# Attention and softplus feed-forward on one core: 64-column transposes, masks in the scores' tile mode, and another order of the first chunk's tasks

## The chip, the cores and the metric

The kernel runs on one core of a Trainium2 chip. Its engines each work through a queue of their own, in the order of the program: TensorE (PE in the profile) with its weight loads (PEld), VectorE (DVE), ScalarE (ACT), GpSimd (POOL) and SyncE (SP), which here only issues DMAs. The metric is device time in microseconds, the median of several runs; lower is better.

## What is computed

The reference is attention with two kinds of masks, followed by a feed-forward layer with a softplus between its two products:

```python
def _attn_ref(q, k, v):                      # 8 batches, 8 heads, 576 positions, 64 wide
    scores = scale * np.matmul(q, k.transpose(0, 1, 3, 2))
    mask_local = (rel >= 0) & (rel < stride)                      # heads 0-3, stride 32
    mask_strided = (rel >= 0) & (pos[None, :] % stride == pos[:, None] % stride)   # heads 4-7
    scores = np.where(masks, scores, -1000000000.0)
    ...
    attn = attn / (np.sum(attn, axis=-1, keepdims=True) + 1e-09)
    return np.matmul(attn, v)

def _moe_ref(x, w_in, w_out):                # x 4608 x 512, w_in 512 x 2048, w_out 2048 x 512
    h = x @ w_in
    g = np.maximum(h, 0.0) + np.log1p(np.exp(-np.abs(h)))
    return g @ w_out
```

The weights come in double precision.

## The kernel before

**Tiling.** Heads are taken in pairs, so there are 32 pairs n (4 to a batch). A query sees at most 64 keys after the host has sorted the positions, so the scores of a pair are nine chunks of 64 columns for 128 query rows, in two parts (six chunks and three). The feed-forward layer takes the 4608 tokens in nine chunks of 512, and the hidden width in 16 blocks f of 128. Each product is done with a high and a low part of both operands: 12 matmuls of 128x512 for a block of the hidden layer (`hidden`), and 12 for its share of the output (`output`).

**Staging.** The first chunk is special. Beside it the 32 weight blocks are brought into two parts, and the first eight pairs go through attention. All this stands as a list of task names, `FIRST`, written out by hand; tasks are emitted in its order, so it sets the order on every engine's queue and on SP's DMA queue. From the second chunk on, a planner (`Plan`) with costs and due times sets the order; nothing of that part is changed.

**Names in `FIRST`.** `q`, `k`, `v`, `wi`, `wo` and a number are loads; `D` lays q out (one half of the heads each, `D00` and `D01`). For a pair n and part j: `S` scores on PE, `X` row maxima on DVE, then either `Y`, `E`, `Z` (subtract, one wide exp, sums) or `x`, `E` (bias, one exp to each chunk, on ACT); `r`, `R`, `M` guard, reciprocal and normalising. `T` and `C` are transposes on PE and their copies out of PSUM (pairs 0 to 3), `P` transposes on DVE (pairs 4 to 7), `V` the product with v, `H` and `L` the high and low part of its result, which is the input x of the feed-forward layer. A weight block goes through `a` (ACT), `B`, `d`, `c` (DVE), `h` (high part) and `l` (low part). `F` is a block of the hidden layer, `A`, `Ae`, `Al`, `u` its softplus, `Gh`, `Gl` its two parts, `O` its share of the output, `y` the result; `Fa0` is the first nine matmuls of `F0`, for pairs 0 to 2. Names starting with `Q` belong to the second chunk. `ON_POOL`, `ON_VECTOR` and `ON_SCALAR` move single tasks from their usual engine.

**What matters around the change.** `F0` needs x of the first 512 tokens, so all of pairs 0 to 3 up to their `L`. PSUM is shared tightly: two buffers `ph` serve the hidden layer and the transposes `T`, one buffer `po` serves `V`. The masks (`mask_b`, 192 KB) are loaded by the first DMA on ACT's queue (L163). In the first two batches the mask is added on PE after a part's scores, by one matmul against the identity over all 128 rows (L336). A transpose group `T` (L447 to L460) zeroes its PSUM buffer and then does 12 matmuls of 32 weight columns each. The result tile `o` (L656) is taken from a pool of four buffers, also for the two halves into which the very last tile is split.

Of the kernel before, what the change touches and what calls it, by code (L numbers as in the profile page):

```python
# [33 lines left out]


FIRST = """
W q0 k0 D01 D00 S00 S01 X00 Y00 q1 D10 X01 D11 x01 E00 Z00 k1 S11 X11 E01 r0 R0 M0 q2 D21 S10
T00 wi0 D20 Y11 X10 x10 ai0 Bi0 T01 di0 k2 E11 S21 Z11 S20 E10 ci0 v0 r1 C00 R1 M1 X21 x21 C01 V00
wo2 q3 ao2 Bo2 do2 co2 D30 hi0 D31 wi2 T02 C02 X20 Y20 k3 H00 L00 ai2 Bi2 E20 ho2 Z20 T10 wi1 di2
v1 E21 r2 T11 S31 V01 X31 S30 lo2 x31 R2 wo3 C10 T12 ci2 H01 L01 X30 Y30 ai1 C11 V10 C12 hi2 E31  # L40
wo0 M2 H10 L10 li2 E30 Z30 T20 C20 li0 r3 R3 ao3 Bi1 M3 T21 V11 C21 H11 L11 wi11 ai11 Bi11 di1 T22
T32 C32 di11 v2 wi3 V20 C22 H20 ci1 ci11 hi11 L20 T31 ai3 Bi3 v3 hi1 li1 C31 T30 C30 li11 wo1 wi4
V21 H21 L21 V31 di3 wo6 ao1 Bo1 ao0 ci3 V30 H31 L31 H30 L30 Fa0 hi3 li3 do1 Bo0 co1 do0 Bo3 q4 D4
wi12 co0 F0 A0 Ae0 ho1 k5 Al0 u0 lo1 Fa1 k4 S40 ai4 wi6 X40 Bi4 x40 ho0 lo0 wi5 Gh0 ai5 wi7 Bi5 F1
A1 Gl0 ai7 Ae1 Al1 E40 do3 co3 di4 u1 Gh1 ho3 lo3 F2 A2 Ae2 Bi7 ci4 di5 O0 q5 wi10 wo5 ao5 Al2 Gl1
wi8 S41 D5 X41 ci5 x41 E41 u2 Gh2 hi5 di7 li5 F3 hi4 A3 Bo5 do5 ci7 Ae3 Al3 r4 R4 li4 co5 O1 M4
S50 X50 x50 hi7 u3 wo12 v4 F5 F4 ho5 Gl2 lo5 Gh3 Gl3 P4 E50 S51 ai6 ai8 Bi8 di8 X51 O2 wo4 ao4 Bi6
wo7 x51 di6 ci6 hi6 A5 Ae5 Al5 u5 li7 Bo4 q6 A4 E51 r5 k6 D6 V40 ci8 do4 O3 H40 L40 S60 co4 R5
wi13 Ae4 ai10 Bi10 Al4 V41 H41 li6 wi9 M5 u4 Gh4 Gl4 X60 Gh5 ho4 x60 L41 P5 F7 F6 hi8 wo15 lo4 Gl5
li8 di10 v5 O4 k7 E60 ao6 Bo6 A7 ai13 S61 A6 Ae6 V50 O5 Al6 ci10 hi10 do6 co6 u6 wo11 wo8 q7 li10  # L50
F10 Ae7 Al7 X61 ho6 ai9 u7 x61 ao7 Bo7 do7 Bi13 di13 Bi9 Gh7 Gl7 ci13 H50 L50 wo14 lo6 di9 ci9 Gh6
Gl6 F8 D7 E61 r6 S70 co7 A10 Ae10 ao8 Al10 Bo8 do8 R6 hi9 A8 wi15 u10 V51 li9 X70 x70 O6 Ae8 Al8
co8 wo9 u8 M6 H51 L51 wi14 P6 ho8 lo8 ai12 Gh8 ho7 lo7 Gl8 F11 hi13 li13 Bi12 Gh10 Gl10 wo10 ao9
Bo9 F9 O7 E70 S71 ai15 Bi15 do9 X71 co9 v6 ao10 Bo10 A9 Ae9 Al9 x71 do10 V60 H60 L60 u9 ho9 A11 q8
lo9 Ae11 Al11 u11 O8 di15 ci15 Gh11 Gh9 Gl9 di12 V61 H61 ao11 Bo11 wo13 F13 hi15 li15 E71 r7 R7 O9
co10 ho10 A13 ci12 hi12 ao13 Ae13 Al13 k8 v7 Gl11 L61 lo10 do11 F15 ao12 O10 M7 co11 li12 ho11
lo11 u13 Gh13 P7 A15 Ae15 Gl13 ai14 Bi14 di14 ci14 F12 hi14 Al15 u15 O11 q9 A12 Ae12 Al12 u12 Bo12
D8 Gh12 V70 Qa0 li14 F14 do12 co12 ho12 Gl12 lo12 O12 Bo13 do13 A14 co13 ho13 lo13 H70 L70 V71
ao14 Bo14 do14 Ae14 co14 Al14 u14 ho14 lo14 O13 H71 L71 Q1 Gh14 v8 Gl14 O14 ao15 Bo15 do15 co15
Gh15 Gl15 ho15 lo15 QA1 Qu1 Qh1 Ql1 Q0 QA0 O15 y1 Ob15 y2 y3 Qu0 Qh0 y0 Ql0 k9  # L60
# [59 lines left out]
def attention_softplus_ffn(  # L120
# [42 lines left out]
    nc.scalar.dma_start(mask_b, masks)  # L163

# [145 lines left out]
    def scores(n, part):  # L310

        b = order[n][0]
        masked = b < 2
# [8 lines left out]
        pss[n, part] = ps
        lo, hi = SPLIT[part]
        for x in range(lo, hi):
            for place in range(2):
# [2 lines left out]
                nc.tensor.matmul(  # L328
                    ps[64 * place : 64 * place + 64, 64 * (x - lo) : 64 * (x - lo) + 64],
                    lhsT=blocks_of(n)[:, c // 32].rearrange("p h l -> p (h l)"),  # L330
                    rhs=k_of(n)[:, c : c + 64],
                    start=x == lo or not masked,
                    stop=not masked,
                )
        if masked:
            nc.tensor.matmul(  # L336
                ps[:, : 64 * (hi - lo)], lhsT=ident_b, rhs=mask_of(n, part), start=False, stop=True
            )
# [103 lines left out]
    def early_transposes(n, g):  # L442

        ph = phs["t", n, g] = ps_h.tile([P, 512], F32, tag="ph", name=f"pt_{n}_{g}")[
            :, : 4 * TILE
        ]
        nc.tensor.matmul(ph, lhsT=warm[:, :P], rhs=warm[:, : 4 * TILE], start=True, stop=False)  # L447
        ph = ph.rearrange("p (h a c) -> p h a c", h=2, a=2)
        for x in range(2):
            for i in range(3):  # L450
                a = 2 * g + x
                chunk, place = (6 + a % 3, a // 3) if i == 1 else (a, i // 2)
                for c in range(2):
                    nc.tensor.matmul(
                        ph[32 * (i + c) : 32 * (i + c) + 32, :, x, 32 * i : 32 * i + 32],
                        lhsT=prob[n % 2][:, chunk, 32 * c : 32 * c + 32],
                        rhs=ident[:, 64 * place : 64 * place + 64],
                        start=False,
                        stop=x == 1 and (c == 0 or i == 2),
                    )  # L460
# [514 lines left out]
```

## Time and profile before

| | us |
|---|---|
| median of three runs (898.67 to 898.98) | 898.88 |
| the profiled execution's own time | 899.74 |
| its span on the chip | 897.5 |
| PE busy in the span | 885.0 (99%) |
| DVE busy | 601.4 (67%) |
| ACT busy | 446.9 (50%) |
| POOL busy | 60.0 (7%) |

The span runs from the first to the last instruction of the profiled execution. A share of busy time is a mean over stages with different limits: PE is at 99% over all, but in the first 35 us it waits several times, and there DVE, ACT and the DMAs are close to full. Where a row says `<-`, the name behind it is what ended the wait. Matmuls overlap, so a row's duration is longer than the distance to the next row; f32 matmuls show as two records each.

### The profile page before, as it was taken

To read this page: it belongs to the slowest core of one execution; us is meant where nothing else is said; L and a number is where in the kernel's file an instruction comes from. 1 tells how busy PE (TensorE), PEld (TensorE's weight loads), DVE (VectorE), ACT (ScalarE), POOL (GpSimd) and SP (SyncE) were. 2 spreads that over 40 slices of the span, in tenths; PEclk is the share of its full clock that TensorE was granted. 3 is DMA by queue.
4 is the path that set the end of the run, shared out by engine and by line. 5 is a ranking of instruction groups with operands and counts; after the bars stand their busy time and mean duration, and the time that the engine had idled before them with its cause. 6 is when DMAs were issued, how large, how long until landed. Compare 5 with 4: busy or idle time off the path is not lost.

```text
span 897.5 us, 14490 instructions
## 1 busy us (share of the span) xinstructions
PE 885.0 (99%) x5700; PEld 723.8 (81%) x5700; DVE 601.4 (67%) x1308; ACT 446.9 (50%) x796; POOL 60.0 (7%) x77
## 2 busy tenths in 40 slices
...
DMA packets 50084, 58.28 MB, mean 65 GB/s; under 512 B 3168, under 2 KB 35296, under 8 KB 50016
## 3 DMA queue, kind: packets, MB, share of 16 engines
...
q10 hardware_dynamic: 288, 0.33, 0.1%
...
## 4 chain that ended last, share of the span: by engine, by line
PE 86%; DVE 6%; ACT 3%; DMA 3%; issue 1%; SPq 1%; POOL 0%; ACTq 0%; POOLq 0%
PE py L647 40%; PE ph L607 39%; PE ps L328 2%; DMA ri<-in_moe_w_in_dram 2%; PE pv L484 2%; DVE pt L432 1%; PE po L484 1%; PE po L328 1%; ACT qT L256 1%; ACT prob L374 1%; DVE u L628 1%; DMA ro<-in_moe_w_out_dram 1%; DVE a_i L561 1%; DVE a_o L561 0%; DVE a_o L578 0%
## 5 line engine op out<-in xcount | busy, mean ns | idle before, releaser
L647 PE MATMUL py<-w_o,gh 128*128 128x512 f32 x1152 | 359.2, 393 | 0.1
L607 PE MATMUL ph<-x_h,w_i 128*128 128x512 f32 x1152 | 355.7, 390 | 1.0 <-DVE u L628 1.0
L619 ACT ACTIVATE u<-ph 128x512 f32<-128x512 f32 x144 | 86.4, 600 | 394.9 <-PE ph L607 391.9
L607 PEld LDWEIGHTS ph<-x_h,w_i 128*128 128x128 f32 x1152 | 215.8, 188 | 46.3 <-DVE u L628 1.6
L647 PEld LDWEIGHTS py<-w_o,gh 128*128 128x128 f32 x1152 | 213.8, 188 | 47.3 <-POOL w_o L593 0.9
L647 PE MATMUL py<-w_o,gl 128*128 128x512 f32 x576 | 224.2, 389 | 0.0
L607 PE MATMUL ph<-x_l,w_i 128*128 128x512 f32 x576 | 224.1, 389 | 0.0
L628 DVE SCALAR_TENSOR_TENSOR u<-ph,u 128x512 f32<-128x512 f32 x144 | 98.9, 688 | 171.9 <-ACT u L624 170.4
L432 DVE STREAM_TRANSPOSE pt<-prob 32x192 f32<-32x192 f32 x448 | 137.1, 314 | 6.4
L647 PEld LDWEIGHTS py<-w_o,gl 128*128 128x128 f32 x576 | 108.1, 188 | 22.8
L607 PEld LDWEIGHTS ph<-x_l,w_i 128*128 128x128 f32 x576 | 108.1, 188 | 22.6
L640 DVE TENSOR_TENSOR gl<-u,gh 128x512 fp32r<-128x512 f32 x138 | 96.1, 697 | 11.2 <-ACT gh L256 0.3
L622 ACT ACTIVATE u<-u 128x512 f32<-128x512 f32 x144 | 91.3, 634 | 4.5
L624 ACT ACTIVATE u<-u 128x512 f32<-128x512 f32 x144 | 90.9, 632 | 4.4
L256 ACT COPY qT<-prob 64x576 f32<-64x576 f32 x56 | 70.5, 1260 | 0.3
L256 DVE CAST gh<-u 128x512 fp32r<-128x512 f32 x130 | 55.4, 426 | 10.6 <-PE py L647 0.5
L391 DVE TENSOR_TENSOR prob<-ps,mask_b 128x384 f32<-128x384 f32 x24 | 13.4, 558 | 50.4 <-PE ps L328 50.4
L328 PEld LDWEIGHTS ps<-kT,qT 128*64 128x64 f32 x720 | 23.6, 137 | 11.6 <-issue 9.9
L328 PE MATMUL ps<-kT,qT 128*64 128x64 f32 x720 | 28.0, 226 | 0.3 <-ACT qT L256 0.3
L484 PE MATMUL pv<-pt,v_in 128*64 128x96 f32 x396 | 22.2, 248 | 0.0
L422 DVE TENSOR_TENSOR prob<-prob,st 128x576 f32<-128x576 f32 x28 | 21.2, 757 | 0.9
L391 DVE TENSOR_TENSOR prob<-po,mask_b 128x192 f32<-128x192 f32 x24 | 8.6, 357 | 19.3 <-ACT x_h L522 19.3
...
## 6 DMA issues: line engine op xcount, KB each, us to landing
...
prob<-in_qk_dram SPq DMA_DIRECT2D x28, 288.0 KB, 2.7
kT<-in_qk_dram SPq DMA_DIRECT2D x28, 288.0 KB, 3.0
...
```

Source lines behind the costliest of these rows:

```text
L256: (engine.copy if engine is nc.scalar else engine.tensor_copy)(dst, src)
L328: nc.tensor.matmul(ps[64 * place : 64 * place + 64, 64 * (x - lo) : 64 * (x - lo) + 64], lhsT=blocks_of(n)[:, c // 32].rearrange("p h l -> ...
L391: nc.vector.tensor_tensor(pv, sv, m, op=ALU.add)
L432: nc.vector.transpose(pt[32 * (i + c) : 32 * (i + c) + 32, h, a : a + hi - lo, 32 * i : 32 * i + 32,], src[:, lo:hi, 32 * c : 32 * c + 32],)
L484: nc.tensor.matmul(po[64 * h : 64 * h + 64, TILE * x : TILE * x + TILE], lhsT=vs[n][:, a, h, :], rhs=pt_of(n, a)[:, h, a % 2], start=True, ...
L607: nc.tensor.matmul(ph, lhsT=w32["i", f][:, half, cc * P : (cc + 1) * P], rhs=x_of(x, cc)[:, t0 : t0 + n], start=(i == 0), stop=(i == 3 * N ...
L619: nc.scalar.activation(us[c, f], phs[c, f], AF.Abs)
L622: nc.scalar.activation(u, u, AF.Exp, scale=-1.0)
L624: nc.scalar.activation(u, u, AF.Ln, bias=1.0)
L628: nc.vector.scalar_tensor_tensor(u, in0=phs.pop((c, f)), scalar=0.0, in1=u, op0=ALU.max, op1=ALU.add)
L640: engine.tensor_tensor(g, us.pop((c, f)), ghs[c, f].bitcast(F32), op=ALU.subtract)
L647: nc.tensor.matmul(py[t], lhsT=g[:, sl], rhs=w32["o", f][:, half], start=(f == 0 and n == 0), stop=(f == NFC - 1 and n == 2),)
```

## The change

There are five edits.

1. **Transposes.** In `early_transposes` a block whose 64 columns land on 64 rows in line is done by one matmul of 64 weight columns; only the block in the middle (i = 1) is still split in two of 32. A group has 8 matmuls after, 12 before.
2. **Masks.** For pairs 1 to 7 the mask is written first, by two matmuls that have 64 output rows each, and the scores are added to it. For pair 0 the two mask matmuls still follow the scores.
3. **The mask load** leaves its place at the head of ACT's queue and becomes a task `mask` in `FIRST`.
4. **The order** `FIRST` and the lists of engines are new throughout.
5. **The last half tile** of the result takes its buffer from the pool of the softplus (`u_pool`), not from the result's four.

```diff
 FIRST = """
-W q0 k0 D01 D00 S00 S01 X00 Y00 q1 D10 X01 D11 x01 E00 Z00 k1 S11 X11 E01 r0 R0 M0 q2 D21 S10
+W wi0 ai0 Bi0 di0 q0 D01 D00 ci0 q1 D11 D10 k0 q3 D30 D31 wo0 mask hi0 ao0 S00 X00 Y00 E00 S01 X01
...
 ON_POOL = """
-D10 D20 D30 ho2 r2 x31 hi11 hi3 x40 ho3 x41 hi5 x50 ho5 hi6 r5 x60 ho6 x61 x71 ho9 ho11 Gh13 hi14
-ho13 ho14
+D30 hi0 D20 x10 x21 x31 hi5 hi8 ho1 hi3 ho5 ho7 x70 hi13 Gh10 Gh13 hi15 ho12 ho13 Gh15 ho14 ho15
 """.split()
 ON_VECTOR = """
-D00 M0 M1 lo2 C12 M3 li1 li3 lo0 Gl0 lo3 Gl1 li5 li4 li7 li6 li10 Gl7 lo6 Gl6 Gl10 Gl9 li15 Gl11
-lo10 M7 Gh12 li14 Gl12 Gl14 Gh15 Gl15
+D01 D11 M0 lo0 M3 li1 C31 li2 li3 Gl0 Gh1 Gl3 li6 Gh4 Gl4 lo5 li9 lo8 Gl10 Gl9 li14 li15 Gl12 lo12
+lo13 Gh14 Gl14 lo14 Gl15 lo15
...
     mask_b = const.tile([P, 12 * 64], BF16, name="mask_b")
-    nc.scalar.dma_start(mask_b, masks)
...
+        rows = [slice(64 * place, 64 * place + 64) for place in range(2)]
+
+        def add(first):
+            for place in range(2):
+                nc.tensor.matmul(
+                    ps[rows[place], : 64 * (hi - lo)],
+                    lhsT=ident_b[:, rows[place]],
+                    rhs=mask_of(n, part),
+                    start=first,
+                    stop=not first,
+                )
+
+
+        if masked and n > 0:
+            add(True)
...
-        if masked:
-            nc.tensor.matmul(
-                ps[:, : 64 * (hi - lo)], lhsT=ident_b, rhs=mask_of(n, part), start=False, stop=True
-            )
+        if masked and n == 0:
+            add(False)
...
-        for x in range(2):
-            for i in range(3):
+
+        for i, width in ((1, 32), (0, 64), (2, 64)):
+            for x in range(2):
                 a = 2 * g + x
                 chunk, place = (6 + a % 3, a // 3) if i == 1 else (a, i // 2)
-                for c in range(2):
+                for c in range(0, 64, width):
+                    lo = 32 * i + c
                     nc.tensor.matmul(
-                        ph[32 * (i + c) : 32 * (i + c) + 32, :, x, 32 * i : 32 * i + 32],
-                        lhsT=prob[n % 2][:, chunk, 32 * c : 32 * c + 32],
+                        ph[lo : lo + width, :, x, 32 * i : 32 * i + 32],
+                        lhsT=prob[n % 2][:, chunk, c : c + width],
...
-        o = io_pool.tile([P, DM], F32, tag="io", name=f"o_{c}_{t}")[:, cols]
+        if cols.start == 0:
+            o = io_pool.tile([P, DM], F32, tag="io", name=f"o_{c}_{t}")[:, cols]
+        else:
+            o = u_pool.tile([P, 512], F32, tag="u", name=f"o_{c}_{t}")[:, : DM - cols.start]
...
+    first["mask"] = lambda: nc.scalar.dma_start(mask_b, masks)
```

What the new list does to the queues shows best at the head of the program. On SP's queue before, the loads began with q and k of the first pairs (`raw_q` and `early_l`), and the first weight block (`ri`) came sixth:

```order
L253 DMA raw_q_153<-in_qk_dram 128x576
L274 DMA early_l_92<-in_qk_dram 128x576
L253 DMA raw_q_181<-in_qk_dram 128x576
L274 DMA early_l_94<-in_qk_dram 128x576
L253 DMA raw_q_205<-in_qk_dram 128x576
L528 DMA ri_235<-in_moe_w_in_dram 128x4x128
```

In the changed program the same place in SP's queue reads:

```order
L541 DMA ri_152<-in_moe_w_in_dram 128x4x128
L251 DMA raw_q_158<-in_qk_dram 128x576
L251 DMA raw_q_163<-in_qk_dram 128x576
L272 DMA early_l_91<-in_qk_dram 128x576
L251 DMA raw_q_168<-in_qk_dram 128x576
L547 DMA ro_172<-in_moe_w_out_dram 128x512
L272 DMA early_l_93<-in_qk_dram 128x576
```

A weight block of 512 KB now goes ahead of q and k of pair 0, three q go ahead of the second k, and a second weight block (`ro`, for `wo0`) is sixth.

At the head of ACT's queue before, with the semaphores that each instruction waits for (`DMAHW` and a number are the eight semaphores that DMAs share in turn):

```order
L161 ACT_TABLE_LOAD
L163 DMA mask_b<-in_masks_dram 128x768
L208 CAST room_113<-ident_b 128x128 [waits Pool_49]
L256 COPY early_h_91<-raw_q_153 64x32x18 [waits DMAHW0_49]
L256 COPY early_h_93<-raw_q_181 64x32x18 [waits DMAHW3_49]
```

And the head of ACT's queue in the changed program:

```order
L160 ACT_TABLE_LOAD
L206 CAST room_112<-ident_b 128x128 [waits Pool_49]
L561 ACTIVATE a_i_154<-ri_152 128x512 [waits DMAHW0_49]
L254 COPY early_h_90<-raw_q_158 64x18x32 [waits DMAHW1_49]
L254 COPY early_h_92<-raw_q_163 64x18x32 [waits DMAHW2_49]
L254 COPY early_h_96<-raw_q_168 64x32x18 [waits DMAHW4_49]
L700 DMA mask_b<-in_masks_dram 128x768 [waits DMAHW5_49]
L561 ACTIVATE a_o_177<-ro_172 128x512
```

The mask's DMA moved behind four instructions that wait for loads of their own, and it waits for semaphore 5, which the sixth DMA of the program (`ro_172`) raises when it has landed.

On DVE's queue before, from its memsets on (`py` holds the scores of pair 0, `st` its statistics):

```order
L256 COPY early_h_91<-raw_q_153 64x18x32
L364 TENSOR_REDUCE st_178<-py_106 128x6
L351 TENSOR_TENSOR prob_104<-py_106,st_178 128x384
L364 TENSOR_REDUCE st_178<-py_107 128x3
L368 TENSOR_SCALAR st_178<-st_178 128x3
```

And the same place on DVE's queue in the changed program:

```order
L565 TENSOR_SCALAR a_i_154<-a_i_154 128x512
L574 SCALAR_TENSOR_TENSOR a_i_154<-ri_152,a_i_154 128x512
L254 COPY early_h_90<-raw_q_158 64x32x18
L591 SCALAR_TENSOR_TENSOR a_i_154<-ri_152,a_i_154 128x512
L254 COPY early_h_92<-raw_q_163 64x32x18
L375 TENSOR_REDUCE st_193<-py_105 128x6
L362 TENSOR_TENSOR prob_103<-py_105,st_193 128x384
L375 TENSOR_REDUCE st_193<-py_106 128x3
```

The three DVE steps of the weight block and a second copy of q stand ahead of the first row maxima now; from there on the first pairs' steps follow in much the same order as before.

More of the change, by code (lines that the diff above doesn't have):

```diff
@@ L36 @@
 FIRST = """
-W q0 k0 D01 D00 S00 S01 X00 Y00 q1 D10 X01 D11 x01 E00 Z00 k1 S11 X11 E01 r0 R0 M0 q2 D21 S10
[L38 to L59, printed above, removed]
@@ L60 @@
-Gh15 Gl15 ho15 lo15 QA1 Qu1 Qh1 Ql1 Q0 QA0 O15 y1 Ob15 y2 y3 Qu0 Qh0 y0 Ql0 k9
+W wi0 ai0 Bi0 di0 q0 D01 D00 ci0 q1 D11 D10 k0 q3 D30 D31 wo0 mask hi0 ao0 S00 X00 Y00 E00 S01 X01
+x01 k1 S11 Bo0 do0 E01 X11 Z00 q2 D20 D21 Y11 r0 S10 X10 x10 wi4 k2 S21 R0 E11 Z11 S20 M0 ai4 Bi4
+co0 di4 E10 T01 C01 T00 C00 k3 r1 ci4 T02 R1 M1 X20 ho0 v0 X21 Y20 wi1 ai1 Bi1 V00 H00 S30 C02 L00
+S31 x21 lo0 wo1 di1 E20 X31 V01 E21 Z20 H01 wi5 L01 T11 C11 li0 ai5 r2 ci1 v2 Bi5 T10 R2 X30 T12
+Y30 C10 hi4 x31 v1 wi8 wi7 V10 H10 L10 C12 M2 di5 E31 V11 ci5 H11 L11 wi2 li4 T21 E30 Z30 r3 R3
@@ new lines @@
+T20 C21 C20 T22 hi1 M3 li1 k4 ai8 Bi8 di8 V20 C22 hi5 H20 L20 T30 C30 v3 ci8 T32 ai2 Bi2 wo3 T31
+C31 wo7 V21 C32 V31 ao1 li5 H21 L21 V30 di2 q4 hi8 wi3 ai3 Bi3 li8 H30 H31 L31 Fa0 L30 F0 wi10 D4
+A0 Ae0 Al0 di3 ci2 Bo1 do1 ci3 wo4 co1 ho1 u0 Fa1 hi2 li2 hi3 S40 X40 x40 q5 ai7 wi9 Bi7 Gh0 F1
+li3 wo2 ao2 Bo2 F2 wo6 E40 S41 ao3 Gl0 do2 wi11 A2 Ae2 Al2 di7 v4 A1 Bo3 Ae1 Al1 do3 co3 u2 O0 lo1
+X41 x41 E41 ci7 hi7 co2 F3 r4 R4 M4 ho2 wo9 u1 Gh1 D5 Gl1 li7 ho3 A3 lo2 F4 k5 wo5 P4 Gh2 wi6 Ae3
+Gl2 Al3 u3 O1 S50 lo3 X50 ao4 q6 ao6 Bo6 x50 wo15 O2 Bo4 Gh3 Gl3 wi15 do4 co4 do6 wo10 wi12 V40
@@ new lines @@
+ai6 Bi6 di6 E50 S51 X51 A4 x51 ci6 co6 H40 L40 F5 Ae4 O3 Al4 u4 ho4 lo4 ai10 wi14 Bi10 hi6 li6 Gh4
+Gl4 F6 di10 ci10 D6 ai11 E51 A5 Ae5 ao5 r5 Bi11 di11 ci11 A6 R5 Bo5 do5 co5 V41 H41 L41 Ae6 Al6 u6
+M5 Al5 u5 hi11 k6 ho5 S60 X60 x60 P5 O4 ho6 lo6 hi10 li10 Gh6 Gl6 F7 E60 Gh5 Gl5 ai9 ao9 lo5 Bi9
+F8 S61 X61 v5 V50 A7 Ae7 Al7 u7 A8 Ae8 li11 di9 O5 Bo9 ci9 do9 x61 co9 F11 Gh7 Al8 u8 q7 Gl7 ao7
+H50 wo8 L50 ao8 Bo8 O6 Bo7 do7 co7 D7 A11 V51 do8 E61 r6 ho7 R6 hi9 Ae11 wi13 Al11 li9 co8 u11 k7
+S70 X70 F10 M6 H51 ho8 lo8 F9 Gh8 Gl8 ao10 x70 L51 lo7 wo12 ao12 Gh11 ho9 lo9 O7 Gl11 E70 S71 v6
```

16 lines of the change are left out of this document (11 added, 5 removed).

## The prediction

> **What bounds the kernel now.** I read the stages first (busy time in stretches of the span: PE, PEld, DVE, ACT, POOL, then the clock, the DMAs' busy share and GB/s), because a share over the whole span says nothing of the first 35 us.
>
> ```profile
> 0.00:10.00 10.00, 8.07 (x85) 4.47 (x85) 6.00 (x12) 5.01 (x9) 7.92 (x25) 1.00 0.84 278
> 10.00:20.00 10.00, 7.51 (x187) 5.45 (x187) 9.18 (x22) 9.06 (x28) 2.19 (x2) 1.00 1.07 394
> 20.00:30.00 10.00, 8.58 (x203) 6.14 (x203) 9.83 (x23) 8.80 (x29) 4.84 (x5) 1.00 1.00 344
> 80.00:120.00 40.00, 40.00 (x232) 32.16 (x231) 39.32 (x86) 32.48 (x75) 17.01 (x16) 1.00 0.33 113
> 120.00:130.00 10.00, 8.99 (x48) 6.80 (x47) 9.74 (x18) 5.57 (x9) 1.97 (x2) 1.00 0.13 36
> 130.00:897.50 767.50, 763.62 (x4560) 631.39 (x4558) 478.60 (x1049) 341.38 (x542) 5.29 (x5) 1.00 0.14 42
> ```
>
> In the lead-in PE has gaps, while DVE is 92 to 98% busy after the first ten us. From 80 us on PE is full, but for 1 us at 120 to 130 and the end of the last stretch. Next come PE's own timeline and its waits:
>
> ```profile
> PE ph L607 <- DVE u L628: 1.0, 1, 1.0
> PE ps L328 <- ACT qT L256: 0.3, 1, 0.3
> ```
>
> ```profile
> 34.09 0.72 PE L484 MATMUL pv<-early_l,room 128*64 128x96 f32 x12 [1.21 <-DVE x_l L520]
> 34.73 0.73 PE L607 MATMUL ph<-x_h,w_i 128*128 128x512 f32 x2
> ...
> 123.86 0.73 PE L607 MATMUL ph<-x_h,w_i 128*128 128x512 f32 x2 [0.99 <-DVE u L628]
> ```
>
> At 34.73 the feed-forward layer begins (`Fa0`), and behind it PE waits only twice, 0.3 and 1.0 us. So the time is **the start of `Fa0`, plus PE's work behind it, plus 1.3 us of waits, plus the tail**. What delays `Fa0` is the row above it: `V30` waited 1.21 us for an `x_l`, which is `L21` on DVE. DVE's timeline of the lead-in:
>
> ```profile
> 4.12 0.87 DVE L256 COPY early_h<-raw_q 64x576 f32<-64x576 f32 x1 [0.20 <-DMA raw_q<-in_qk_dram]
> 7.23 0.56 DVE L364 TENSOR_REDUCE st<-py 128x6 f32<-128x384 f32 x1 [2.24 <-PE py L336]
> ...
> 10.47 0.17 DVE L414 TENSOR_SCALAR st<-st 128x9 f32<-128x9 f32 x1 [0.41 <-ACT prob L374]
> ...
> 12.44 0.17 DVE L368 TENSOR_SCALAR st<-st 128x6 f32<-128x6 f32 x1
> 12.52 0.42 DVE L552 TENSOR_SCALAR a_i<-a_i 128x512 uint32<-128x512 uint32 x1
> 12.98 0.69 DVE L561 SCALAR_TENSOR_TENSOR a_i<-ri,a_i 128x512 uint32<-128x512 uint32 x1
> ...
> 13.85 1.49 DVE L578 SCALAR_TENSOR_TENSOR a_i<-ri,a_i 128x512 uint32<-128x512 uint32 x1
> ...
> 15.70 0.76 DVE L422 TENSOR_TENSOR prob<-prob,st 128x576 f32<-128x576 f32 x1
> ...
> 31.90 1.76 DVE L593 TENSOR_TENSOR w_i<-a_i,w_i 128x512 fp32r<-128x512 f32 x1
> 33.59 0.44 DVE L520 TENSOR_TENSOR x_l<-pv,x_h 128x288 fp32r<-128x288 f32 x1
> ```
>
> DVE waits 2.24 us for the first scores with their mask (`X00` at 7.23), then works without a break, 0.41 us apart, to the end of `L21` at 34.03. That is a chain of 26.8 us, and the first mask matmul starts it.
>
> **The lead-in, and the one large term.** In the new order DVE does the same things between `X00` and `L21`: all maxima, subtractions and sums of pairs 0 to 3, five weight blocks in full and the first step of a sixth, two low parts, one copy out of PSUM. Off DVE are `M1` (0.76 us in the row at 15.70) and `x10` and `x21` (0.17 each, the row at 12.44); `r2` comes to DVE at the 0.17 of the row at 10.47. So the chain loses 0.9 us and is 25.9 us long. `M1` on POOL costs more, but its result is wanted only by the transposes of pair 1, whose `L10` stands some 8 us further down DVE's queue; that covers it.
>
> The head of the chain moves much more. `X00` needs the first mask matmul, and that needs `mask_b`.
>
> ```profile
> 0.76 0.39 ACTq L163 DMA_DIRECT2D mask_b<-in_masks_dram  x1
> ```
>
> ```profile
> 3.05 6.32 DMA ri<-in_moe_w_in_dram
> ```
>
> ```profile
> prob<-in_qk_dram SPq DMA_DIRECT2D x28, 288.0 KB, 2.7
> ...
> mask_b<-in_masks_dram ACTq DMA_DIRECT2D x1, 192.0 KB, 3.5
> ```
>
> Before, the mask was issued at 0.76 and landed 3.5 us later, ahead of the scores. Afterwards its DMA waits until `wo0` has landed, the sixth load on SP's queue. When is that? Before, q0 landed at 4.1 (end of the wait in front of DVE's copy) and the sixth load, `wi0`, at 3.05 + 6.32 = 9.37: five loads, four of 288 KB and one of 512 KB, in 5.25 us. The new order puts a 512 KB load first, issued at about 0.75. Before, 480 KB (q0 and the mask side by side) took until 4.1 from about the same start, so I take 4.2. Behind it come four loads of 288 KB and one of 512 KB again: 4.2 + 5.25 = 9.4. At the 394 GB/s of the best stretch above those 1.70 MB need 4.3 us, so 8.5 is the low bound. The mask, 3.5 us after its issue, lands at 12.9.
>
> ```profile
> 5.38 1.55 PE L328 MATMUL py<-early_l,early_h 128*64 128x64 f32 x24 [0.60 <-ACT early_h L256]
> 6.86 0.34 PE L336 MATMUL py<-mask_b,ident_b 128*128 128x384 bf16 x1
> ```
>
> Before, `X00` began 7.23 - 6.86 = 0.37 us behind the mask matmul; so 13.3 against 7.23, **6.0 us later**. The scores themselves are no bound: k0 is fourth in the queue, lands near 6.9, and they end about 8.5. Nor is DVE's work put in front: `Bi0`, `di0`, `D01`, `ci0`, `D11` are 0.42 + 0.69 + 0.87 + 0.69 + 0.87 = 3.5 us from about 4.9, over by 8.5. DVE then stands idle for nearly 5 us with `X00` at the head of its queue, and PE stands at the mask matmul with all other scores queued behind it. So `L21`, and `Fa0` with it, come 6.0 - 0.9 = **5.1 us later**. The bounds: issue at 8.5 and the 2.7 us of the nearest quicker load give `X00` at 11.6, and +3.5.
>
> A sentence on a page: the Trainium skill ("DMA: Bandwidth & Descriptors", "Anatomy of one DMA") fits a DMA at about 2.0 us plus its bytes at 436 GB/s, an estimate of 2.45 us for the mask; the trace has 3.5 us, and by the page the lead-in term would be 4.1.
>
> **Transposes.** Twelve groups lose 4 of 12 matmuls each. I cost this at nothing: PE waits in the lead-in as it is, and DVE's chain sets its end. The cover is that chain; without it a group's 24 records (0.67 us by the timeline, as the one below) would become 16, up to 0.2 us each, 2.7 us in all at the very most.
>
> ```profile
> 24.47 0.67 PE L454 MATMUL pt<-room,prob 128*32 128x64 f32 x24
> ```
>
> **Masks.** Eight mask additions (pairs 4 to 7) stand between dense matmuls on PE and count in full.
>
> ```profile
> 46.68 0.39 PE L647 MATMUL py<-w_o,gl 128*128 128x512 f32 x1
> 47.00 0.57 PE L328 MATMUL ps<-kT,qT 128*64 128x64 f32 x12
> 47.50 0.26 PE L336 MATMUL ps<-mask_b,ident_b 128*128 128x192 bf16 x1
> 47.54 0.70 PE L607 MATMUL ph<-x_h,w_i 128*128 128x512 f32 x2
> 48.08 0.39 PE L607 MATMUL ph<-x_l,w_i 128*128 128x512 f32 x1
> ```
>
> Between the records at 46.68 and 48.08 lie 1.40 us; three dense records of 0.227 (0.68) leave 0.72 for scores and mask, of which the scores have 0.50 from start to mask. The mask and all changes of shape come to 0.22. Two half matmuls instead of one could run side by side and save the change in the middle (down to -0.1 us each), or one after the other (up to +0.13, half of the 0.26). I take +0.02 each, 0.2 in all; the ends are -0.8 and +1.0. The Trainium skill ("TensorEngine Tiling (Array Packing)", "Key Properties") says that changing the tiling mode drains TensorE; by that this edit saves one drain a block. The row's 0.22 leaves room for no more than the -0.8 above.
>
> **Waits behind `Fa0`.** DVE has done one weight block more by `L21` (0.42 + 0.69 + 0.69 = 1.8 us, now ahead of `X00`), and in the lists two `Gl` and `M7` leave DVE for about as much in biases and one `Gh`. It is some 2 us less behind PE than before, so the 1.0 us wait at 123.86 should go: -1.0. The other wait, 0.3, I leave.
>
> **Tail.**
>
> ```profile
> 893.66 0.42 DVE L256 COPY o<-py 128x256 f32<-128x256 f32 x1 [0.67 <-PE py L647]
> 894.38 0.37 ACT L256 COPY o<-py 128x256 f32<-128x256 f32 x1 [0.81 <-DMA out_dram<-o]
> ```
>
> The last half tile on ACT waits for a result buffer whose DMA is still under way, until 894.38; its DVE twin began at 893.66. With a buffer of its own it begins 0.7 us sooner. What is late next is the twin's own DMA, issued 0.2 us or so sooner than ACT's was: I take -0.5.
>
> **Sum**, against the profiled execution's own 899.74: +5.1 - 1.0 + 0.2 - 0.5 = +3.8, 903.5. That execution was 0.86 above the median of the three runs (898.88), so I forecast a median of **902.7 us**. A difference of about 0.2%, 1.8 us, is what a measurement of this kernel can tell from none.
>
> **The rivals.** (1) *The mask is not late* and the weight block in front pays: slower turns into no change. For it speaks that DVE has real work for the 3.5 us ahead of `X00`; against it the semaphore on which the DMA waits. If the mask lands by 8.5, `X00` follows the scores at 9.1, 1.9 later than before; less 0.9 the lead-in is +1.0, the sum -0.3, the median 898.6. Each us that the mask lands behind 8.5 adds one; from 10.6 on it is slower by over 1.8. (2) *The DVE holds go.* Two DVE operations took 1.49 and 1.76 us where their like took 0.69, while POOL was at work: 1.9 us that the new order may or may not meet again. Without them the forecast is 900.8. Against it: POOL has more large operations in the lead-in now (`M1`, `li0`, `M2`, `li4`). Together (1) and (2) give 896.7, faster. (3) *A new wait in the dense part:* in the new queue `u1` stands behind `u2` and a row of weight steps, and the fifth hidden block needs the buffer that `u1` frees; at some three weight steps late (0.69 each) this adds 2 us: 904.7. (4) *The transposes do nothing*, since the added change from 32 to 64 columns takes back what the four matmuls give; that is already the forecast's zero.
>
> **How the numbers follow.** Forecast 0.50 (nearly all of it slower, 0.04 within 0.2%: its own bounds, +3.5 for the lead-in and -0.8 for the masks, end at 900.1); (3) 0.10, slower; (2) 0.12, half slower, half same; (1) 0.16, of which 0.12 same and 0.04 faster; (1) with (2) 0.12, faster. That makes faster 0.16, same 0.22, slower 0.62. The range reaches from between the case (1) and its faster form, 897.5, to 905.0, which takes in (3).
>
> **What would show it.** Right: the first row maxima on DVE near 13.3 us with a wait of nearly 5 us before it, ended by the mask matmul or its DMA; ACT's issue of the mask near 9.4; the first 128x512 matmul of the hidden layer near 39.8; no wait for `u` near 125; ACT's last copy without a wait for a DMA. Wrong: `X00` before 11, or `Fa0` before 37. If `Fa0` is late as said and the time is not, PE's work behind it must have become shorter, and the masks would be the place to look.

## The result and the profile after

| | before | after |
|---|---|---|
| median, same chip and hour (us) | 898.93 (898.67 to 900.03) | 907.79 (907.29 to 908.44) |
| span of the profiled execution (us) | 897.5 | 906.4 |
| first row maxima, `X00` (us) | 7.23 | 15.41 |
| start of the feed-forward layer, `Fa0` (us) | 34.73 | 42.57 |
| start of the last matmul (us) | 893.24 | 901.91 |

The changed kernel takes 1.0094 times as long (95% interval 1.0082 to 1.0106), 8.9 us more. The direction was forecast; the size was not: 902.7 was named, and 905.0 was the upper end.

The stages of the changed kernel, with the columns of the prediction's first table (busy time of PE, PEld, DVE, ACT, POOL, then the clock granted to PE as a share of full speed, the DMAs' share and GB/s):

```profile
0.00:10.00 10.00, 5.14 (x32) 2.44 (x33) 5.55 (x10) 5.97 (x6) 6.88 (x25) 1.00 0.81 280
10.00:20.00 10.00, 4.47 (x69) 4.12 (x70) 4.47 (x13) 4.00 (x11) 1.81 (x3) 1.00 1.09 382
20.00:30.00 10.00, 10.00 (x183) 7.73 (x179) 8.07 (x20) 7.39 (x29) 2.81 (x4) 1.00 0.98 352
80.00:120.00 40.00, 38.54 (x241) 29.45 (x241) 39.18 (x84) 33.25 (x85) 20.55 (x19) 1.00 0.34 116
```

From 10 to 20 us PE, DVE and ACT are idle for more than half of the time, where DVE was at 92% before; the DMAs alone are at full load. Then PE is full for ten us, catching up. At 80 to 120 us, where PE had been at 40.00 of 40, it now misses 1.5 us.

The head of the program on ACT, PE and DVE in turn (start, length, engine and line; in brackets the wait and what ended it):

```profile
9.73 0.38 ACTq L700 DMA_DIRECT2D mask_b<-in_masks_dram  x1
```

```profile
7.84 1.55 PE L341 MATMUL py<-early_l,early_h 128*64 128x64 f32 x24 [3.06 <-DMA early_l<-in_qk_dram]
14.84 0.53 PE L326 MATMUL py<-mask_b,ident_b 128*64 128x384 bf16 x2 [5.46 <-DMA mask_b<-in_masks_dram]
15.12 0.90 PE L341 MATMUL py<-early_l,early_h 128*64 128x64 f32 x12
```

```profile
7.67 0.66 DVE L254 COPY early_h<-raw_q 64x576 f32<-64x576 f32 x1
15.41 0.56 DVE L375 TENSOR_REDUCE st<-py 128x6 f32<-128x384 f32 x1 [7.08 <-PE py L326]
```

The scores were done at 9.4; PE stood 5.46 us for the mask, and DVE 7.08 us for PE. The chain of waits names it too:

```profile
3.18 6.53 DMA ro<-in_moe_w_out_dram
...
9.73 5.07 DMA mask_b<-in_masks_dram
...
14.84 0.53 PE py L326 x2
```

ACT issued the mask at 9.73, once `wo0` (`ro`) had landed, as the prediction said (9.4). But the mask then needed 5.07 us to land, not 3.5.

PE's waits behind `Fa0`, where there were 1.0 for `u` and 0.3 before:

```profile
PE ph L620 <- DVE u L641: 0.6, 1, 0.6
PE ps L326 <- ACT prob L385: 0.4, 1, 0.4
PE pv L497 <- DVE pt L443: 0.3, 1, 0.3
PE ph L620 <- POOL w_i L606: 0.2, 1, 0.2
PE py L660 <- POOL w_o L606: 0.2, 1, 0.2
PE py L660 <- DVE w_o L606: 0.2, 1, 0.2
```

Two waits, 1.3 us in all, became six small ones for three engines, 1.9 in all. At the end, DVE's and ACT's last copies:

```profile
902.34 0.42 DVE L254 COPY o<-py 128x256 f32<-128x256 f32 x1 [0.67 <-PE py L660]
```

```profile
902.80 0.37 ACT L254 COPY o<-py 128x256 f32<-128x256 f32 x1 [0.55 <-DVE o L254]
```

ACT's half no longer waits for a result DMA, but it now waits for DVE's half: it begins 0.89 us behind the start of the last matmul, 1.14 before, and the span's end is no nearer (4.49 us behind that start, 4.26 before): the DMA that takes this half out landed 2.0 us after its issue, 1.7 before.

So the 8.9 us of the span are +7.84 up to `Fa0`, +0.83 between `Fa0` and the last matmul (859.34 against 858.51), and +0.23 behind it.

### The profile page after: what moved, and what is told of

It is laid out like the page before. It is cut to its first block, busy times and chain, and to the rows that moved or that the text cites. A ratio compares the mean times of both kernels' runs of the same rounds, so it can differ in the third digit from the quotient of the medians.

```text
span 906.4 us, 14334 instructions
## 1 busy us (share of the span) xinstructions
PE 888.1 (98%) x5620; PEld 726.9 (80%) x5620; DVE 601.9 (66%) x1311; ACT 446.6 (49%) x793; POOL 61.8 (7%) x77
## 4 chain that ended last, share of the span: by engine, by line
PE 92%; DVE 4%; DMA 2%; ACT 1%; issue 1%; POOL 0%; SPq 0%; ACTq 0%
PE py L660 42%; PE ph L620 41%; PE ps L341 2%; PE pv L497 2%; PE po L497 1%; DMA ro<-in_moe_w_out_dram 1%; PE po L341 1%; DVE pt L443 1%; PE pt L467 1%; PE py L341 1%; DMA mask_b<-in_masks_dram 1%; DVE a_i L574 0%; DVE a_o L591 0%; DVE u L641 0%; ACT qT L254 0%
## 5 line engine op out<-in xcount | busy, mean ns | idle before, releaser
L653 DVE TENSOR_TENSOR gl<-u,gh 128x512 fp32r<-128x512 f32 x136 | 94.1, 692 | 11.6 <-DVE gh L254 0.9
L417 ACT ACTIVATE prob<-prob 128x576 f32<-128x576 f32 x24 | 16.5, 689 | 9.1 <-DVE prob L411 9.1
```

The lines of the kernel that those rows point to most:

```text
L653: engine.tensor_tensor(g, us.pop((c, f)), ghs[c, f].bitcast(F32), op=ALU.subtract)
```

## The experiments

Each time stands beside that of the kernel before in the same session (899.35 for the first four, 899.63 for the next four, then 899.94, 899.8 and 899.65).

**1. The changed kernel with the mask's DMA first on ACT's queue.**

```diff
-W wi0 ai0 Bi0 di0 q0 D01 D00 ci0 q1 D11 D10 k0 q3 D30 D31 wo0 mask hi0 ao0 S00 X00 Y00
+mask W wi0 ai0 Bi0 di0 q0 D01 D00 ci0 q1 D11 D10 k0 q3 D30 D31 wo0 hi0 ao0 S00 X00 Y00
```

> The changed kernel with the mask's DMA back at the head of ACT's queue, nothing else. If the late mask is the cause of the loss: the scores of pair 0 end near 9.5 us with the mask already there, the first row maxima come near 10.2 instead of 15.4, the feed-forward layer starts near 37.4 instead of 42.6, and the time is about 902.6, some 5 below the changed kernel and still 3.7 above the one before, because a weight block stands ahead of q and k. If the rest of the order is the cause, and the mask only one wait among several: above 905.

Measured 903.0, ratio 1.0038 (1.0023 to 1.0053); its span is 901.2, so the mask's place costs 5.2 of the span's 8.9 us, and 3.7 remain. `Fa0` begins at 37.42, 5.15 sooner, and `X00` at 10.24, 5.17 sooner: an early `X00` carries through one for one here.

**2. The kernel before with its mask late**, behind the first copies on ACT.

```diff
-    nc.scalar.dma_start(mask_b, masks)
...
-W q0 k0 D01 D00 S00 S01 X00 Y00 q1 D10 X01 D11 x01 E00
+W q0 k0 q1 D01 D00 D10 D11 mask S00 S01 X00 Y00 X01 x01 E00
```

> The kernel before, with the mask's DMA moved on ACT's queue behind the two copies of q, as in the changed kernel it stands behind copies. It does not wait for a weight block here, so it is issued near 6 us, with several loads issued on SP ahead of it. If a DMA in this stretch takes the 5 us that it took in the changed kernel: landing near 11, first row maxima near 11.4 (before 7.2), time about 902.7. If it takes the 3.5 us that the prediction used: landing near 9.5, first row maxima near 9.9, time about 901.3. If the mask's place does not matter: 898.9.

Measured 904.5, ratio 1.0056 (1.0041 to 1.0071), over all the expectations. (`q1`, `D10` and `D11` stand earlier in this list too, but the engines and SP do everything else in the same order as before.) On ACT, PE and DVE:

```profile
5.56 0.39 ACTq L683 DMA_DIRECT2D mask_b<-in_masks_dram  x1
```

```profile
11.91 0.48 PE L335 MATMUL py<-mask_b,ident_b 128*128 128x384 bf16 x1 [5.73 <-DMA mask_b<-in_masks_dram]
```

```profile
12.42 0.56 DVE L363 TENSOR_REDUCE st<-py 128x6 f32<-128x384 f32 x1 [8.03 <-PE py L335]
```

Issued 4.8 us later than in the kernel before, the mask landed 6.3 us after its issue, and `X00` came 5.2 us later. `Fa0` came 4.7 us later (39.39). A late mask alone makes the kernel slower, in the old order too.

**3. The kernel before with every other edit** (64-column transposes, masks first and in halves, the last half tile from `u_pool`), its own order, and the mask early.

```diff
+mask W q0 k0 D01 D00 S00 S01 X00 Y00 q1 D10 X01 D11 x01 E00 Z00 k1 S11 X11 E01 r0 R0 M0 q2 D21 S10
...
+        for i, width in ((1, 32), (0, 64), (2, 64)):
```

> The changed kernel with the order and engine lists of the one before and the mask's DMA at the head: 64-column transposes, masks in the scores' tile mode and the last half tile's buffer alone. If all of the loss is in the order: 898.9 within 1 us. By the trace of the changed kernel a transpose group takes 1.00 us against 0.95, a masked block about 0.1 us more, and the tail ended 0.2 us later: together about +1, 899.9. If the edits give what they look like, 4 of 12 matmuls a group less and one change of shape less: 897.5.

Measured 899.42, ratio 0.9999 (0.9990 to 1.0008). In the old order the other edits sum to nothing, so the loss comes with the new order, the mask's place in it included. That they cost nothing within the new order too was not tried.

**4. The changed kernel with PE kept busy** by 14 matmuls of no use between the first scores and the mask.

```diff
         if masked and n == 0:
+            if part == 0:
+                dummies(14)
             add(False)
```

> The changed kernel with 14 matmuls of 128x512 that write an unused tile, between the scores of pair 0 and their mask, so that PE works through its wait for the mask. If PE runs slow after the wait because it stood idle (the scores behind it took 1.54 us instead of 0.9, transposes 1.28 instead of 0.81): the scores take 0.9 us at once, the wait of DVE for the transposes near 25.7 us shrinks from 1.9 us, the feed-forward layer starts 1 to 2 us sooner, time about 906.3. If the slowness there has no effect on the end: 907.8.

Measured 907.49, ratio 1.0090 (1.0073 to 1.0107). The scores right behind the mask on PE:

```profile
15.37 0.54 PE L341 MATMUL py<-early_l,early_h 128*64 128x64 f32 x12
```

They take 0.54 where the changed kernel took 0.90 (the row at 15.12 above), and `Fa0` begins at 41.59, 0.98 sooner. But the loss falls from 8.9 us only to 8.1, which the two intervals don't tell apart: a slow start of PE after the wait is at most a small part of the loss.

**5. Mask early, and q0 and k0 ahead of the weight block.**

```diff
-mask W wi0 ai0 Bi0 di0 q0 D01 D00 ci0 q1 D11 D10 k0 q3 D30 D31 wo0 hi0 ao0 S00 X00 Y00 E00 S01 X01
-x01 k1 S11
+mask W q0 D01 D00 k0 S00 X00 Y00 E00 S01 X01 x01 q1 wi0 D11 D10 ai0 Bi0 di0 ci0 q3 D30 D31 wo0 hi0
+ao0 k1 S11
```

> The changed kernel with the mask's DMA first on ACT, q0 and k0 ahead of the first weight block on SP, and the steps of that block (B, d, c on DVE) behind the first row maxima. Theory (what is left of the loss once the mask is early, some 3.7 us, is the weight block ahead of q and k): X00 near 7.5 us instead of 8 to 10; but the 1.8 us of that block's steps and a copy of q come back into DVE's chain behind X00, so Fa0 falls from 37.4 only to about 36 and the time to 901.5. Rival A (the head is all of it): Fa0 near 35, 900. Rival B (the order of DVE's work, one weight block more before Fa0, is all of it, and the head costs nothing): Fa0 stays near 37.4 and the time at 903.

Measured 903.64, ratio 1.0044 (1.0030 to 1.0057). DVE and PE in this run:

```profile
6.95 0.56 DVE L375 TENSOR_REDUCE st<-py 128x6 f32<-128x384 f32 x1 [1.83 <-PE py L326]
...
10.42 0.43 DVE L565 TENSOR_SCALAR a_i<-a_i 128x512 uint32<-128x512 uint32 x1 [1.15 <-ACT a_i L561]
```

```profile
37.81 0.73 PE L620 MATMUL ph<-x_h,w_i 128*128 128x512 f32 x2
```

`X00` is earlier than in the kernel before, and `Fa0` is about where it was in run 1: by its numbers rival B. It is not a clean test, since the block's steps were not taken away but moved behind `X00`, and PE's clock was low in this profile (last section).

**6. One word of the changed kernel: the mask on SP's queue**, at the same place of the order.

```diff
-    first["mask"] = lambda: nc.scalar.dma_start(mask_b, masks)
+    first["mask"] = lambda: nc.sync.dma_start(mask_b, masks)
```

> The changed kernel with one word other: the mask's DMA stands at the same place of the order but on SP's queue, right behind the load of wo0, so it is issued near 4 us and not behind a wait for wo0. Theory (loads are served about in the order in which they were issued, whatever the queue; on ACT the mask came behind all that SP had issued by 9.7 us): the mask lands right behind wo0, near 10 us, the first row maxima at about 10.5 instead of 15.4, Fa0 near 38, time 903 to 903.5. Rival (the mask's transfer itself is slow, about 5 us behind any start among busy loads, or X00 was held by something else): X00 stays later than 13, time over 905.5.

Measured 903.29, ratio 1.0038 (1.0024 to 1.0051).

```profile
3.66 0.43 SPq L700 DMA_DIRECT2D mask_b<-in_masks_dram  x1
```

```profile
10.82 0.53 PE L326 MATMUL py<-mask_b,ident_b 128*64 128x384 bf16 x2 [0.77 <-DMA mask_b<-in_masks_dram]
```

The mask still stands behind `wo0` in the list, but its DMA is issued at 3.66 and not at 9.73, and it is there at 10.8 and not at 14.8. The span is 901.5: 4.9 us come back. The cost was not where the task stood in the list, but that on ACT's queue the issue waited for loads to land, and then came behind all that SP had issued meanwhile.

**7. The 64-column transposes alone**, in the kernel before.

> The kernel before with the 64-column transposes alone. The prediction's zero: DVE's chain covers PE in the lead-in, and a group's 8 matmuls with two changes of shape take as long as 12 of one shape (1.00 against 0.95 us a group in the traces): within 0.3 us of the kernel before. If the four matmuls saved were to count, 12 groups by up to 0.2: up to 2.7 us sooner.

Measured 899.73, ratio 0.9999 (0.9991 to 1.0008). Nothing, as costed.

**8. `M1`, `x10` and `x21` on POOL**, in the kernel before: one term of the prediction by itself.

```diff
-D10 D20 D30 ho2 r2 x31
+D10 D20 D30 ho2 r2 x10 x21 x31
...
-D00 M0 M1 lo2
+D00 M0 lo2
```

> The kernel before with M1, x10 and x21 moved from DVE to POOL, as in the changed kernel. This tests the prediction's term of -0.9 us for DVE's shorter chain by itself: by it Fa0 begins 0.9 us sooner (33.8) and the time falls by 0.9 to 1.9 us (the wait for u behind it may shrink too), 897 to 898.5. Rival: POOL takes longer (1.2 to 1.4 us for M1) and its results, or the holds of DVE while POOL runs, give the gain back: Fa0 at 34.5 to 35, time within 0.3 us of before.

Measured 900.02, ratio 1.0002 (0.9993 to 1.0011), and `Fa0` at 35.33, 0.6 later. On POOL and on DVE:

```profile
15.48 1.16 POOL L422 TENSOR_TENSOR prob<-prob,st 128x576 f32<-128x576 f32 x1 [2.52 <-DVE st L418]
...
16.96 1.80 POOL L256 COPY early_h<-raw_q 64x576 f32<-64x576 f32 x1
```

```profile
14.91 0.17 DVE L414 TENSOR_SCALAR st<-st 128x9 f32<-128x9 f32 x1 [0.48 <-ACT prob L374]
...
16.25 0.67 DVE L552 TENSOR_SCALAR a_o<-a_o 128x512 uint32<-128x512 uint32 x1 [0.37 <-ACT a_o L548]
...
17.68 1.63 DVE L578 SCALAR_TENSOR_TENSOR a_o<-ro,a_o 128x512 uint32<-128x512 uint32 x1
```

DVE has less to do and gets to the next things sooner, where it waits for ACT (0.48, 0.37). The long step has only moved: the step L578 that took 1.49 us before (the prediction's row at 13.85) takes 0.68 here, and that of the next block takes 1.63, while POOL's copy runs, where it took 0.69 before. The 1.1 us taken from DVE are gone. That `Fa0` is later still can't be put down to the edit alone, as PE's clock shows 0.83 at 10 to 20 us in this profile and 1.00 in that of the kernel before.

**9 to 11. A weight block's steps moved behind `Fa0`**: in run 9 those of `wi8` in the kernel of run 1 (behind `F1`), in runs 10 and 11 those of `wi11` in the kernel before (behind `F2` and `F5`). Run 11:

```diff
-wi11 ai11 Bi11 di1 T22 T32 C32 di11 v2 wi3 V20 C22 H20 ci1 ci11 hi11 L20
+wi11 di1 T22 T32 C32 v2 wi3 V20 C22 H20 ci1 L20
...
-C31 T30 C30 li11 wo1 wi4
+C31 T30 C30 wo1 wi4
...
-u3 wo12 v4 F5 F4
+u3 wo12 v4 F5 ai11 Bi11 di11 ci11 hi11 li11 F4
```

> The changed kernel with the mask first on ACT, and all steps of weight block wi8 (a, B, d, c, h, l), which stood ahead of Fa0, moved behind F1; F8 needs them much later. Theory (what is left of the loss with an early mask, some 3 us, is DVE's work ahead of Fa0: one weight block more than before, 1.8 us on DVE, and idle gaps): Fa0 near 35.6 instead of 37.4, and since DVE makes up the block behind Fa0 where PE waits little, time 901 to 901.5. Rival (DVE is full until 125 us, so what is taken from ahead of Fa0 comes back as a wait for u behind it): Fa0 near 35.6, but a longer wait of PE for DVE there, time 902.5 to 903.5.

> The kernel before with all steps of weight block wi11 moved from ahead of Fa0 to behind F2. The same theory: Fa0 1.8 us sooner or more (its two long DVE holds of 1.5 to 1.8 us stood there), near 32.5; time near 897.5 if DVE makes it up while PE has work. Rival (DVE full until 125 us): the wait for u near 124 grows from 1.0 by as much, time 899 to 900, no change.

> As the last, with the steps of wi11 behind F5. Theory: the same start of Fa0 near 32.5 and the same or a little better time, 897.5. Rival (DVE full until 125 us): the place within that stretch does not matter, and the wait for u takes it back: 899 to 900.

Measured 907.2 (ratio 1.0081, 1.0067 to 1.0095), 902.58 (1.0027, 1.0017 to 1.0038) and 901.07 (1.0012, 1.0003 to 1.0020). `Fa0` came at 36.64, 34.03 and 32.47. PE's waits behind `Fa0` of run 11:

```profile
PE ps L328 <- ACT qT L256: 1.5, 1, 1.5
PE py L647 <- POOL gl L640: 1.4, 1, 1.4
PE ph L607 <- DVE u L628: 1.0, 1, 1.0
```

`Fa0` began 2.3 us sooner than in the kernel before, and the time did not fall: PE lost 2.6 us more behind it, to ACT and POOL. In run 9 the one wait `PE ps L326 <- ACT prob L385` grew from 0.4 to 3.1 us. In run 10 the longest new wait is for DVE after all, for its step `gl`, and ACT comes next (1.0 us):

```profile
PE py L647 <- DVE gl L640: 2.0, 1, 2.0
```

The start of `Fa0` is not a term by itself; what is put behind it comes back there. The wait for `u`, which the rivals named, hardly grows (1.4 in run 10, 1.0 in run 11). The moved steps include those on ACT (`a`, `h`), so these runs don't test DVE's work alone.

**12 and 13. The three DVE steps of two weight blocks left out**, in the kernel before and in that of run 1. Both then leave out part of the computation, and serve for their times alone.

```diff
     def w_shift(w, f):
+        if w + str(f) in ("i11", "o2"):
+            return
```

> The kernel before without the three DVE steps (B, d, c) of the weight blocks i11 and o2, which are left out altogether, not moved: some 2 x 1.6 = 3.2 us less DVE work ahead of Fa0. Theory (DVE is full to 125 us and its work up to there counts, wherever it stands): Fa0 near 32, the wait for u near 124 does not grow, time 896 to 897.5, 2.5 to 3.5 us less. Rival (what brings the time back behind Fa0 is another engine, ACT or POOL): Fa0 near 32 too, but waits for ACT or POOL behind it, time 898.5 to 900.

> The changed kernel with the mask first on ACT, without B, d and c of the weight blocks i8 and o0 (left out, not moved). Theory (the 3.7 us that are left come from DVE's work and gaps up to 125 us): Fa0 near 34.2, time about 3 us below the 903.0 with them, near 900. Rival (the order makes PE wait for ACT and POOL behind Fa0): time stays over 902.

Measured 898.22 (ratio 0.9982, 0.9974 to 0.9991) and 902.56 (1.0028, 1.0017 to 1.0039). With some 3.2 us of DVE's work gone, run 12 is 1.6 us faster than the kernel before (0.7 in the profiled spans). Run 13's profiled span is 0.5 shorter than run 1's (900.7 against 901.2), but run 1's had a lower clock: where the mean granted clock was 1.000, run 13 took 902.27 to 902.74 and run 1 902.21 and 902.80, which is no gain. `Fa0` begins at 34.12 in run 12, 0.6 sooner than before, and at 36.97 in run 13, 0.45 sooner than in run 1, where the theories had 32 and 34.2. DVE in run 12:

```profile
32.96 0.46 DVE L520 TENSOR_TENSOR x_l<-pv,x_h 128x288 fp32r<-128x288 f32 x1 [1.43 <-ACT x_h L522]
```

DVE now waits 1.43 us for ACT. So DVE, 92 to 98% busy from 10 to 30 us in the kernel before, was not the only bound: ACT, busy for 9.8, 8.6 and 8.9 of the ten us from 10, 20 and 30 us in this run, stood right behind it.

**14. Two steps of block `i5` moved behind pair 3's normalising**, in the kernel of run 1; the chain of waits showed them ahead of it.

```diff
-M2 di5 E31 V11 ci5 H11 L11 wi2 li4 T21 E30 Z30 r3 R3 T20 C21 C20 T22 hi1 M3 li1 k4
+M2 E31 V11 H11 L11 wi2 li4 T21 E30 Z30 r3 R3 T20 C21 C20 T22 hi1 M3 di5 ci5 li1 k4
```

> The changed kernel with the mask first on ACT (903.0), and the two DVE steps of weight block i5 (d, c), which stand ahead of pair 3's sums and normalising, moved behind M3. Theory (they lie on the chain that sets Fa0): the normalising of pair 3 begins near 29.6 instead of 31.67, Fa0 near 35.3 instead of 37.4, and since no work moves past Fa0, time near 901. Rival (as in the runs with moved weight blocks, an earlier Fa0 is given back by later waits for ACT, POOL or DVE): Fa0 near 35.3, time 902.5 to 903.5. Second rival (ACT's or PE's part of the chain sets it anyway): Fa0 stays over 36.7.

Measured 904.04, ratio 1.0042 (1.0028 to 1.0055); `Fa0` at 38.05. DVE:

```profile
28.50 0.46 DVE L533 TENSOR_TENSOR x_l<-pv,x_h 128x288 fp32r<-128x288 f32 x1 [1.25 <-ACT x_h L535]
...
29.96 0.76 DVE L433 TENSOR_TENSOR prob<-prob,st 128x576 f32<-128x576 f32 x1
...
33.44 1.65 DVE L574 SCALAR_TENSOR_TENSOR a_i<-ri,a_i 128x512 uint32<-128x512 uint32 x1
35.01 0.45 DVE L533 TENSOR_TENSOR x_l<-pv,x_h 128x288 fp32r<-128x288 f32 x1
```

The normalising began at 29.96 instead of 31.67, as expected, but the moved steps then stood ahead of the next low part at 35.01 (34.01 in run 1), for which PE waited 1.0 us. The gain was lost a few rows further down the same queue. `Fa0` stayed over 36.7, as the second rival had it. That the median is 1.0 above run 1's is not the edit: three of the five executions had a mean granted clock of 0.996 and took 904.04 to 904.19, the two at 1.000 took 902.74 and 902.79, and run 1's two at 1.000 took 902.21 and 902.80.

## Why the prediction went wrong

The four terms, by the prediction's own steps, against the spans:

| term | predicted | measured |
|---|---|---|
| `X00` later | +6.0 | +8.18 |
| chain from `X00` to `Fa0` shorter | -0.9 | -0.34 |
| waits behind `Fa0`, and masks | -1.0 + 0.2 | +0.83 |
| tail | -0.5 | +0.23 |
| sum | +3.8 | +8.9 |

Of the 5.1 us that were missed, 2.2 are in the first term, 0.6 in the second, 1.6 in the third and 0.7 in the last.

**The lead-in's mechanism was right, its size was not.** ACT's issue at 9.73 against 9.4, the wait at the mask, `X00` standing idle behind it: all as said. The step that failed is "The mask, 3.5 us after its issue, lands at 12.9": it took 5.07 us and landed at 14.80. The 3.5 came from the issue at 0.76, when next to nothing stood ahead of it. The profile of the kernel before had a row with the price of the busy stretch, for a load of a quarter of the mask's size (the small loads of v in the lead-in):

```profile
room<-in_v_dram SPq DMA_DIRECT2D x4, 48.0 KB, 7.2
```

SP's queue in the changed kernel, its first issue, the last ahead of the mask's, and the next:

```profile
0.73 0.43 SPq L541 DMA_DIRECT2D ri<-in_moe_w_in_dram  x1
...
8.48 0.39 SPq L290 DMA_DIRECT2D room<-in_v_dram  x1
10.45 0.38 SPq L541 DMA_DIRECT2D ri<-in_moe_w_in_dram  x1
```

By 9.73 SP had issued 11 loads for attention and weights and two of v: four of q and four of k (288 KB each), two of `wi` and one of `wo` (512 KB each), and 320 and 48 KB of v, 4208 KB in all. With the mask's 192 KB that makes 4.51 MB. The windows show 280 GB/s up to 10 us and 382 from there: 2.80 MB, then 1.71 MB in 4.5 us, so 14.5 for the end of it all, and the mask landed at 14.80. This sum fits, though with run 6 it fits less well (2.42 MB at 285 GB/s would be there at 8.5, and the mask was at 10.8), so it is a reading and not a law. An estimate of the same kind (bytes issued by the mask's issue, itself included, less what the windows show as moved by then) gives 0.49, 1.8, 2.2 and 1.9 MB still to come in the kernel before, the changed one, run 2 and run 6, where the mask took 3.5, 5.07, 6.3 and 7.1 us from issue to landing. So this time grows with what is under way, but not in proportion. Issuing the mask 6 us sooner, on the queue of the loads, was worth 4.9 us all the same (run 6). Of the 2.2 us by which the first term was too small, the landing is 1.6; the rest are the later issue (0.33) and the slower PE behind the wait (0.57 from mask to `X00`, 0.37 before). The Trainium skill's fit ("DMA: Bandwidth & Descriptors", "Anatomy of one DMA"), 2.0 us plus the bytes at 436 GB/s, gave an estimate of 2.45 us. That section measured it for DMAs that GpSimd issues, and the mask's is issued by ACT or SP; no run shows a landing of the mask that fast.

**"So the chain loses 0.9 us" failed.** It lost 0.34. The prediction took the lead-in for one chain on DVE that works without a break. In the changed kernel the chain of waits stands on PE from the mask matmul at 14.84 up to 31.46, and DVE waits for PE in the middle of it:

```profile
25.71 0.56 DVE L362 TENSOR_TENSOR prob<-py,st 128x384 f32<-128x384 f32 x1 [1.88 <-PE pt L467]
```

Pair 2's subtraction overwrites the tile that pair 0's transposes read, and PE was late with these. In run 4, where PE was kept busy ahead of this stretch, the wait is gone and the chain from `X00` to `Fa0` is 26.00 us, 1.5 shorter than the 27.50 before. Run 8, which makes just this edit in the kernel before, gained nothing: what DVE sheds it waits for ACT, or gives back while POOL works. Nor is `X00` a strict head of the chain there: in the profiles of runs 3 and 7, whose order is that of the kernel before, it came at 6.72 and 7.65, and `Fa0` at 34.65 and 34.72. The rival that the long DVE steps go failed too; they moved. In the changed kernel:

```profile
32.29 1.45 DVE L574 SCALAR_TENSOR_TENSOR a_i<-ri,a_i 128x512 uint32<-128x512 uint32 x1
...
35.33 1.20 DVE L425 TENSOR_SCALAR st<-st 128x9 f32<-128x9 f32 x1
```

Their like take 0.69 and 0.16.

**"The 1.0 us wait at 123.86 should go: -1.0" failed.** It only shrank to 0.6, and waits for ACT, POOL and other DVE work came in beside it. The prediction counted DVE's work alone, and left the other wait of 0.3 as the only one; runs 9 to 11 show how easily this stage makes new ones.

**"A buffer of its own ... -0.5" failed**: ACT's copy lost one wait and found the next, for DVE's copy out of the same tile `py`: 0.25 us gained there and none at the end, as its DMA took 0.3 longer. In run 3, which has the same edit, the tail is 4.23 us (4.26 before). Whether that wait comes through `py` or through the new buffer was not tried.

**Transposes at nothing were right; the masks' +0.2 priced one kind of block of two.** Run 7 (transposes) and run 3 (all edits) are within 0.1 us of the kernel before. In run 3 the masks are the only edit that falls between `Fa0` and the last matmul, and this stretch takes 858.52 us against 858.51. Below that sum its eight blocks differ, each taken from the last dense matmul ahead to the second record of the dense matmuls behind. In four of them the dense matmuls follow at once, as in the block that the prediction priced (1.40 us, in run 3 1.44): these take 0.04 to 0.08 us more. No change of shape is saved there, since the mask (128*128) had the shape of the dense matmuls behind it, and now has that of the scores (128*64). In the other four a product `V` of 128*64 follows, so the old mask stood as a change in the middle and back. The same place in the kernel before and in run 3:

```profile
78.54 0.26 PE L336 MATMUL ps<-mask_b,ident_b 128*128 128x192 bf16 x1
78.73 0.72 PE L484 MATMUL pv<-pt,v_in 128*64 128x96 f32 x12
```

```profile
78.10 0.52 PE L342 MATMUL ps<-kT,qT 128*64 128x64 f32 x12
78.45 0.66 PE L498 MATMUL pv<-pt,v_in 128*64 128x96 f32 x12
```

This block takes 1.94 us instead of 2.22, the other of its size 1.93 instead of 2.22, and the two larger ones 0.06 and 0.09 less. That a change of tiling mode drains TensorE (the Trainium skill, "TensorEngine Tiling (Array Packing)", "Key Properties") agrees with these rows; but the edit saves none or two changes a block, and not "one drain a block". PE's work gets some 0.5 us shorter, and its waits behind `Fa0` get 0.4 longer (1.7 in run 3, 1.3 before), so nothing is gained.

**The rivals.** "The mask is not late" gave 898.6, which assumed that the weight block in front would then pay. Run 1 takes the lateness away and stands at 903.0, so this rival was wrong by some 4 us even on its own condition. The new wait in the dense part came in another form: six small waits, 0.6 us more in all, and none of 2 us. What holds the last 3.7 us stays open. They come with the order (run 3); putting the first q and k ahead (run 5), taking DVE's work away (run 13) and moving two steps in DVE's queue (run 14) did not bring them back. Some 0.5 go with the clock: run 1's two executions at a mean granted clock of 1.000 stand 3.2 above the kernel before. Of the 3.7 the spans of run 1 show 2.7 as a later `Fa0` and about 1 behind it. The prediction read the lead-in as one chain on DVE. Runs 8, 12 and 14 show DVE and ACT taking turns in it, and in run 1 too DVE stands 1.55 us for pair 0's transposes, which the kernel before doesn't have. So an order has to be judged by all its queues at once, which a sum of one engine's steps can't do.

No version here beats the kernel before; the only faster run, 12, leaves work out.
